# Two decode layers with cached attention: the fold's sums on GpSimd, a thinned chain, and unread products on TensorE behind its norms

## The chip, the cores and the metric

The kernel runs on one core of one Trainium2 chip. The metric is device time in microseconds (us) from launch to the end; lower is better. The core has TensorE (PE; its weight loads are listed apart as PEld), VectorE (DVE), ScalarE (ACT), GpSimd (POOL) and SyncE (SP), which here issues all the loads. Each engine takes its instructions in program order, and semaphores order them between engines. The stated time is the median of 3 runs.

## The reference

Eight sequences (B = 8) decode one token with D = 512. The same pair of blocks is applied twice, with the same weights and the same key and value caches. The caches are bf16 of 8 x 8 x 8192 x 128; a (sequence, head) pair holds 2 MB of keys and 2 MB of values.

```
def _A_ref(x, k_cache, v_cache, wq, wo):
    q = (lambda x, *d: x.transpose(*d))((x @ wq).reshape(B, Sq, Hq, Dh), 0, 2, 1, 3)   # 32 heads of 128
    k = jnp.repeat(k_cache, rep, axis=1)                                               # 8 cached heads, rep = 4
    v = jnp.repeat(v_cache, rep, axis=1)
    scores = jnp.einsum("bhqd,bhkd->bhqk", q, k) * (Dh ** -0.5)
    p = _softmax(scores, axis=-1)
    o = jnp.einsum("bhqk,bhkd->bhqd", p, v)
    return (lambda x, *d: x.transpose(*d))(o, 0, 2, 1, 3).reshape(B, Sq, Hq * Dh) @ wo

def _B_ref(x, w1, w2):                                                                 # 512 -> 1792 -> 512
    return jnp.einsum("bsf,fd->bsd", _silu(jnp.einsum("bsd,df->bsf", x, w1)), w2)

x = A_x
x = x + _A_ref(_layernorm(x, axis=-1), A_k_cache, A_v_cache, A_wq, A_wo)
x = x + _B_ref(_layernorm(x, axis=-1), B_w1, B_w2)
x = x + _A_ref(_layernorm(x, axis=-1), A_k_cache, A_v_cache, A_wq, A_wo)
x = x + _B_ref(_layernorm(x, axis=-1), B_w1, B_w2)
return x
```

## The kernel before

**Tasks.** One task is the attention of one sequence over one cached head in one layer: 128 tasks. `make_tasks` (L146) writes their order down. Of each sequence's eight heads, three (heads 0 to 2) have their keys loaded in both layers; five (heads 3 to 7, the 20 "kept" granules) keep their keys in SBUF from the first layer to the second. The order for a sequence b is: its five kept tasks of layer 0; then five or six other tasks, namely layer-1 tasks of heads 0 to 2 of the sequence before and layer-0 tasks of heads 0 to 2 of the sequences to come; then its five kept tasks of layer 1, which load values alone.

**Chain.** Between the kept tasks of layer 0 and those of layer 1 stands the *chain* of sequence b (`chain_of`, L808): the last wo heads, the residual, a layer norm, w1, silu, w2, the residual, the next layer norm and wq, for one sequence alone. It is a list of small stages.

**Positions.** A task is eight positions (p) of the loop at L857; two positions make a granule of 512 KB of keys or values. Each position emits, in this order: the queries of a task about to begin (`emit_q`), the transposes of key granules up to p + LT (`emit_t`, a VectorE transpose in place), at odd p the score products (`emit_s`, PE, L543), at odd p the products with the values of the granule LP = 14 positions back (`emit_pv`, PE, L608), the fold's steps, the softmax steps of the task before by phase p % 8 (`soft`, L843: maximum at 0, shift and exp at 2, sum at 4, transposes of P at 5, reciprocal at 7), then stages of the chain, or (outside the kept tasks of layer 1) one wo head, then `emit_norm`, and the loads whose slot the planner has free by then. The number of chain stages in a position is the number left over the number of positions left until EARLY = 4 before the first layer-1 kept task, rounded up (L881). Positions order the instructions on each engine; they set no time of their own.

**Loads.** The arena has 27 slots of 512 KB. `plan_loads` (L177) gives each granule a due position and a slot: keys are due LT positions before their first score products, values when `emit_pv` reads them. SP issues them in the order of their due positions and waits for the last reader of the slot. With 20 slots kept, seven circulate.

**Fold.** PV leaves in a PSUM bank (OTp) 128 x 512 partial results, of which each partition owns one of four blocks of 128 columns. `emit_own` (L621, at the position after the last PV, p - LP - 8) copies them to E: for 88 tasks by one ScalarE copy (L624), and for the 40 kept tasks of layer 1 (`eased`) by four VectorE instructions that multiply with the 0/1 column own_x and add (L629, L632). `emit_fold` (L636, two positions later) sums across partitions on PE in fp32: four products with `sel` for a ScalarE copy (eight PE instructions in the profile, L640), one with `hm` for an eased task (two PE instructions, L645). `emit_norm` (three positions after `emit_own`) scales on VectorE. E exists once; OTp, P^T (PT), scores (SCp) and the PSUM bank of the transposes (TPp, NTP = 2) twice. All eight PSUM banks are used.

**Layer norm.** `ln_stages` (L658) has three stages: the sum over the partition's elements on VectorE and the sum across partitions on GpSimd; centring, squares and sum on VectorE, then GpSimd again; variance, a bit-trick seed, three Newton steps and the scaling on VectorE (L685 to L699 for one sequence). In a chain two empty stages (`idle`, SETTLE = 2) follow each norm. `project` (L714) emits w1 and w2 in two pieces of 56 products and wq in four of 32.

Of the kernel before, what the change touches and what calls it, by code (L numbers as in the profile page):

```python
# [5 lines left out]
HQ = 32  # L6
DH = 128
SM_SCALE = DH ** -0.5
LN_EPS = 1e-5
RSQRT_SEED = float(0x5F3759DF)  # L10
# [6 lines left out]
KEEP = 20  # L17
LT = 2
PRE = 10
LP = 14  # L20
EARLY = 4
WO_FROM = 36
NTP = 2
NSCP = 2
# [8 lines left out]
PAIR_ALL = False  # L33
FOLD = 3
FOLD_AT = 2
ACT_FOLD = True
NQS = 4
CW = 32
SETTLE = 2

# [183 lines left out]
def _build(ctx, nc, A_x, A_k_cache, A_v_cache, A_wq, A_wo, B_w1, B_w2, out):  # L224
# [28 lines left out]
    def sb(shape, dt, name):  # L253
        _cnt[0] += 1
        return ctx.enter_context(nc.sbuf_tensor(f"{name}_{_cnt[0]}", shape, dt))
# [38 lines left out]
    s1 = sb([128, B], FP32, "s1")  # L294
    s1a = sb([128, B], FP32, "s1a")
    xc = sb([128, KT, B], FP32, "xc")
    sq = sb([128, KT, B], FP32, "sq")
# [25 lines left out]
    TPp = [ps_bank("TPp", BF16) for _ in range(NTP)]  # L323
    MISC = ps_bank("MISC")
    QSp = ps_bank("QSp")

# [60 lines left out]
    with nc.Block() as block:  # L387

        @block.sync
        def _(sync_eng):  # L390
# [184 lines left out]
            def softmax_sum(ti):  # L575
                st = ti % NST
                op(dve, lambda: dve.tensor_scalar(  # L577
                    ssm[st][:, :], hm[:, :], rs[st][:, 0:1], None, op0=ALU.mult),
                   reads=["hm", f"rs{st}"], writes=[f"ssm{st}"])
                op(pool, lambda: pool.partition_all_reduce(ssa[st][:, :], ssm[st][:, :], 128, bass.bass_isa.ReduceOp.add),  # L580
                   reads=[f"ssm{st}"], writes=[f"ssa{st}"])
# [34 lines left out]

            def eased(ti):
                layer, _b, g = tasks[ti]
                return layer == 1 and (g, 0) in kept

            def emit_own(ti):  # L621
                ob = ti % 2
                if not eased(ti) and ACT_FOLD:
                    op(act, lambda: act.copy(E[:, :], OTp[ob][:, :]), reads=[f"OT{ob}"], writes=["E"])  # L624
                    return
                for x in range(CPB):
                    ot = OTp[ob][:, x * DH:(x + 1) * DH]
                    if x == 0:
                        op(dve, lambda: dve.tensor_scalar(E[:, 0:DH], ot, own_x[:, 0:1], None, op0=ALU.mult),  # L629
                           reads=[f"OT{ob}", "own_x"], writes=["E"])  # L630
                    else:
                        op(dve, lambda x=x, ot=ot: dve.scalar_tensor_tensor(  # L632
                            E[:, 0:DH], ot, own_x[:, x:x + 1], E[:, 0:DH], op0=ALU.mult, op1=ALU.add),
                           reads=[f"OT{ob}", "own_x", "E"], writes=["E"])

            def emit_fold(ti):  # L636
                ob = ti % 2
                if not eased(ti) and ACT_FOLD:
                    steps = [
                        lambda x=x: pe.matmul(OTp[ob][:, 0:REP], E[:, x * DH:(x + 1) * DH], sel[:, x, :],  # L640
                                              start=(x == 0), stop=(x == CPB - 1))
                        for x in range(CPB)
                    ]
                else:
                    steps = [lambda: pe.matmul(OTp[ob][:, 0:REP], E[:, 0:DH], hm[:, :], start=True, stop=True)]  # L645
                mm_group(steps, reads=["E", "hm", "sel"], writes=[f"OT{ob}"])
# [11 lines left out]
            def ln_stages(xv, rx, n):  # L658

                xcv, sqv, xnv = xc[:, :, 0:n], sq[:, :, 0:n], xnT[:, :, 0:n]  # L660

                def first():
# [19 lines left out]
                def third():  # L682
# [7 lines left out]
                       reads=["yr"], writes=["yr"])  # L690
                    if n == 1:
                        scale = 1.0
                        for _n in range(NEWTON):
                            op(dve, lambda: dve.tensor_scalar(t, y, y, v, op0=ALU.mult, op1=ALU.mult),  # L694
                               reads=["yr", "vr"], writes=["tr"])
                            op(dve, lambda: dve.tensor_scalar(y, t, -3.0 * scale ** 2, y, op0=ALU.add, op1=ALU.mult),  # L696
                               reads=["tr", "yr"], writes=["yr"])
                            scale *= -2.0 * scale ** 2
                        op(dve, lambda: dve.tensor_scalar(xnv, xcv, y, 1.0 / scale, op0=ALU.mult, op1=ALU.mult),  # L699
                           reads=["xc", "yr"], writes=["xnT"])  # L700
                        return
                    for _n in range(NEWTON):
# [56 lines left out]

            settle = [idle] * SETTLE  # L760

            def block_stages(xs, rxs, n, fine=False):

                x0, x1, x2 = xs
                r0, r1, r2 = rxs
                parts = 2 if fine else 1

# [11 lines left out]
                def attended():  # L779
                    add_residual(x1, r1, x0, r0, n, CW if n == 1 else n)  # L780

                st = [attended] + ln_stages(x1, r1, n) + settle
                st += joined(project(w1_sb, "w1", FT, KT, lambda k: xnT[:, k, 0:n], "xnT", n, parts), expo)
                st += [silu, idle]
                st += joined(
                    project(w2_sb, "w2", KT, FT, lambda k: hsT[:, k * n:(k + 1) * n], "hsT", n, parts),
                    lambda: add_residual(x2, r2, x1, r1, n, n))
                return st

# [9 lines left out]
            def query(n, dst_of, rdst, parts=1):  # L799
                return joined(  # L800
                    project(wq_sb, "wq", HQ, KT, lambda k: xnT[:, k, 0:n], "xnT", n, parts),
                    lambda: op(
                        dve,
                        lambda: dve.tensor_copy(dst_of, MISC[:, 0:HQ * n].rearrange("p (h b) -> p h b", b=n)),
                        reads=["MISC"], writes=rdst,
                    ))

            def chain_of(b):  # L808
                xs = [XT[n][:, :, b:b + 1] for n in range(3)]
                st = block_stages(xs, ["XT0", "XT1", "XT2"], 1, True)  # L810
                st += ln_stages(xs[2], "XT2", 1) + settle
                return st + query(1, QT2[b % 2][:, 0:HQ].rearrange("p (h b) -> p h b", b=1), [f"QT2_{b % 2}"], 4)

# [41 lines left out]
            ntask = len(tasks)  # L855

            for p in range(NG + LP + GPT + FOLD + 1):  # L857
                tq = (p + LQ) // GPT
# [7 lines left out]
                if p % GPG == GPG - 1 and p < NG:  # L866
                    emit_s(p)
                if p % GPG == GPG - 1 and 0 <= p - LP < NG:
                    emit_pv(p - LP)
# [10 lines left out]
                if chain:  # L880
                    left = max(1, first1[chain_b[0]] - EARLY - p)  # L881
                    for _n in range(-(-len(chain) // left)):
                        chain.pop(0)()
                elif p >= WO_FROM and heads[turn[0]] and not (p < NG and tasks[p // GPT][0] and (tasks[p // GPT][2], 0) in kept
                                             and turn[0] < B):
                    add_heads(turn[0])
# [63 lines left out]
```

## Time and profile before

| What | Value |
|---|---|
| median of 3 runs (lowest to highest) | 1202.7 us (1202.06 to 1204.01) |
| the profiled execution's own time | 1203.2 us |
| its span, first to last instruction | 1201.2 us |
| mean granted TensorE clock | 0.600 |
| busy share PE, PEld, DVE, ACT, POOL | 68%, 42%, 61%, 23%, 10% |
| loaded by the program's queue | 465.12 MB, 99.2% of the span |
| L466 DVE key transposes | 352 of 1240 ns, 436.0 us |
| L608 PE products with the values | 2048 of 549 ns, 283.0 us |
| L543 PE score products | 7040 of 301 ns, 275.6 us |
| L640 PE fold after a ScalarE copy | 704 of 333 ns, 147.9 us |
| L624 ACT copy to E | 88 of 592 ns, 52.1 us |
| L629, L632 DVE to E, eased tasks | 40 of 323 ns, 120 of 351 ns, 55.0 us |
| L577 DVE ssm | 128 of 202 ns, 25.9 us |
| L721 PE w1, w2, wq (wq shown) | 1152 of 185 ns, 35.5 us |

The span is one execution under the hardware profiler; its own time lies 2.0 us over the span. A group's busy time is the union of its instructions; PE's overlap, so 549 ns a product is not what a row of them costs. The rate (GB/s) is what the 16 DMA engines moved in a slice or window, and the clock is TensorE's granted share of full speed.

### The profile page before, as it was taken

Reading aid. Unit: us, or ns where it says so; the run is one execution under the profiler, and the core shown is the slowest. Engines: PE = TensorE matmul, PEld = TensorE weight load, DVE = VectorE, ACT = ScalarE, POOL = GpSimd, SP = SyncE. Lnnn points to the kernel's source line nnn. Section 1 sums busy time; section 2 is a strip of 40 time slices with the busy share of each in tenths; the row PEclk is TensorE's granted clock in tenths of the full one; section 3 lists DMA queues with packets and bytes.
Section 4 is the critical chain, followed back from the end, with each engine's and each line's share of the span. In section 5 each row is a group of like instructions: output and inputs, shape, how many; then the busy total and the mean of one; then the engine's idle time right before and its main releaser. Section 6 shows DMA issues by size and latency. Waiting matters only on the chain.

```text
span 1201.2 us, 32533 instructions
## 1 busy us (share of the span) xinstructions
PE 811.5 (68%) x13960; PEld 505.4 (42%) x13960; DVE 735.7 (61%) x1858; ACT 274.0 (23%) x482; POOL 117.9 (10%) x300
## 2 busy tenths in 40 slices
PE   1537777576856686677757786667757676667865
PEld 1324444344524463345424454345434453345534
DVE  3736665767575655667476756657466756667472
ACT  0212123122312223221312132122312232121321
POOL 0000111001100111001100111001100111001100
PEclk9655576555855576555855566556755676555665
DMA  9999999999999999999999999999999999999993
GB/s 363 385 396 407 399 376 409 408 403 379 396 409 408 392 357 410 408 399 383 400 409 403 393 391 409 409 392 365 403 408 397 365 396 409 408 404 385 385 409 133
DMA packets 131568, 467.19 MB, mean 389 GB/s; under 512 B 13904, under 2 KB 19808, under 8 KB 130912
## 3 DMA queue, kind: packets, MB, share of 16 engines
q1 hardware_dynamic: 131424, 465.12, 99.2%
q8 instruction: 109, 1.79, 0.6%
q14 instruction: 35, 0.29, 0.1%
HBM read 465.05 MB, written 0.01 MB: 387 GB/s over the span
## 4 chain that ended last, share of the span: by engine, by line
DMA 59%; PE 15%; SPq 15%; DVE 7%; issue 3%; ACT 1%; POOL 1%; POOLq 0%; ACTq 0%; DVEq 0%
DMA arena<-in_A_v_cache_dram 48%; SPq L356 15%; DMA arena<-in_A_k_cache_dram 10%; PE OTp L608 5%; PE OTp L640 3%; PE MISC L721 3%; DVE arena L466 3%; PE SCp L543 3%; ACT P L570 1%; PE TPp L589 1%; DVE E L632 1%; DVE tr L694 1%; DVE yr L696 1%; DVE rowmax L554 0%; PE MISC L739 0%
## 5 line engine op out<-in xcount | busy, mean ns | idle before, releaser
L466 DVE STREAM_TRANSPOSE arena<-arena 128x1024 int32<-128x1024 int32 x352 | 436.0, 1240 | 239.1 <-DMA arena<-in_A_k_cache_dram 238.8
L608 PE MATMUL OTp<-arena,PT 128*16 128x512 bf16 x2048 | 283.0, 549 | 292.8 <-DMA arena<-in_A_v_cache_dram 289.9
L570 ACT ACTIVATE P<-SCp,shift 128x512 bf16<-128x512 f32 x128 | 180.4, 1409 | 646.2 <-PE SCp L543 234.1
L543 PE MATMUL SCp<-arena,QB 128*32 128x128 bf16 (+1 forms) x7040 | 275.6, 301 | 3.7 <-DVE mine L563 2.3
L608 PEld LDWEIGHTS OTp<-arena,PT 128*16 128x16 bf16 x2048 | 54.9, 97 | 383.6 <-DMA arena<-in_A_v_cache_dram 375.6
L543 PEld LDWEIGHTS SCp<-arena,QB 128*32 128x32 bf16 x7040 | 167.6, 122 | 63.8 <-issue 41.3
L640 PEld LDWEIGHTS OTp<-sel,E 128*128 128x128 f32 x704 | 140.3, 296 | 37.8 <-issue 25.6
L640 PE MATMUL OTp<-sel,E 128*128 128x4 f32 x704 | 147.9, 333 | 0.9 <-ACT E L624 0.7
L559 POOL PARTITION_ALL_REDUCE tops<-top x128 | 47.5, 371 | 563.1 <-DVE QT L655 241.6
L580 POOL PARTITION_ALL_REDUCE ssa<-ssm x128 | 55.2, 432 | 444.9 <-DVE ssm L577 423.4
L554 DVE TENSOR_REDUCE rowmax<-SCp 128x1 f32<-128x512 f32 x128 | 84.6, 661 | 21.4 <-PE SCp L543 20.9
L593 ACT COPY PT<-TPp 128x256 bf16<-128x256 bf16 x128 | 47.6, 372 | 211.7 <-PE TPp L589 211.7
L589 PE MATMUL TPp<-ident,P 128*128 128x128 bf16 x512 | 70.2, 283 | 12.4 <-ACT P L570 11.8
L589 PEld LDWEIGHTS TPp<-ident,P 128*128 128x128 bf16 x512 | 39.7, 121 | 66.2 <-issue 38.4
L577 DVE TENSOR_SCALAR ssm<-hm,rs 128x4 f32<-128x4 f32 x128 | 25.9, 202 | 66.5 <-ACT P L570 66.5
L624 ACT COPY E<-OTp 128x512 f32<-128x512 f32 x88 | 52.1, 592 | 4.1 <-PE OTp L608 4.1
L739 PEld LDWEIGHTS MISC<-at,wo 128*128 128x128 bf16 x1024 | 33.0, 105 | 34.2 <-DVE at L655 28.8
L721 PE MATMUL MISC<-xnT,wq 128*128 128x32 bf16 (+1 forms) x1152 | 35.5, 185 | 16.9 <-DVE xnT L708 15.7
L632 DVE SCALAR_TENSOR_TENSOR E<-OTp,own_x,E 128x128 f32<-128x128 f32 x120 | 42.1, 351 | 4.3
L721 PEld LDWEIGHTS MISC<-xnT,wq 128*128 128x128 bf16 x1152 | 34.4, 105 | 24.4 <-issue 22.1
L739 PE MATMUL MISC<-at,wo 128*128 128x32 bf16 x1024 | 38.2, 187 | 6.6 <-issue 1.3
L645 PE MATMUL OTp<-hm,E 128*128 128x4 f32 x80 | 20.5, 327 | 24.1 <-DVE E L632 24.1
(61 smaller groups left out, 359.3 us busy)
## 6 DMA issues: line engine op xcount, KB each, us to landing
arena<-in_A_v_cache_dram SPq DMA_DIRECT2D x512, 512.0 KB, 11.2
arena<-in_A_k_cache_dram SPq DMA_DIRECT2D x352, 512.0 KB, 14.9
wq<-in_A_wq_dram SPq DMA_DIRECT2D x1, 4096.0 KB, 16.4
wo<-in_A_wo_dram SPq DMA_DIRECT2D x1, 4096.0 KB, 26.0
w<-in_B_w_dram SPq DMA_DIRECT2D x2, 1792.0 KB, 22.6
P<-in_A_x_dram SPq DMA_DIRECT2D x1, 8.0 KB
out_dram<-P SPq DMA_DIRECT2D x1, 8.0 KB
```

The costliest lines, as they stand in the source:

```text
L356: eng.dma_start(out_ap, in_ap).then_inc(counter.sem, 16)
L466: op(dve, lambda: dve.transpose(words, words), reads=[r_half(slot, 0), r_half(slot, 1)], writes=[r_half(slot, 0), r_half(slot, 1)])
L543: lambda n=n, t=t, lo=lo, hi=hi, of=of: pe.matmul(SCp[bank][t * QUAD:(t + 1) * QUAD, lo * 128:hi * 128], QB[qn][:, n, :], of(t, n), start= ...
L554: op(dve, lambda: dve.tensor_reduce(rowmax[:, :], SCp[bank][:, :], AX.X, ALU.max), reads=[f"SC{bank}"], writes=["rowmax"])
L570: op(act, lambda: act.activation(P[:, :].rearrange("p (x j k) -> p k x j", x=CPB, k=NGRAN), SCp[bank][:, :].rearrange("p (k x j) -> p k x ...
L580: op(pool, lambda: pool.partition_all_reduce(ssa[st][:, :], ssm[st][:, :], 128, bass.bass_isa.ReduceOp.add), reads=[f"ssm{st}"], writes=[f ...
L589: lambda c=c: pe.transpose(tpv[:, c, :], P[:, c * 128:(c + 1) * 128], ident[:, :])
L608: lambda t=t: pe.matmul(OTp[ob][t * QUAD:t * QUAD + CPB * REP, :], PT[pb][:, k, t].rearrange("p x r -> p (x r)"), ARENA[:, slot * SLOT + t ...
L632: op(dve, lambda x=x, ot=ot: dve.scalar_tensor_tensor(E[:, 0:DH], ot, own_x[:, x:x + 1], E[:, 0:DH], op0=ALU.mult, op1=ALU.add), reads=[f" ...
L640: lambda x=x: pe.matmul(OTp[ob][:, 0:REP], E[:, x * DH:(x + 1) * DH], sel[:, x, :], start=(x == 0), stop=(x == CPB - 1))
L721: lambda o=o, k=k: pe.matmul(MISC[:, o * n:o * n + w], w_sb[:, k, o * 128:(o + 1) * 128], rhs_of(k).to_broadcast([128, w]) if n == 1 else ...
L739: lambda o=o, h=h: pe.matmul(MISC[:, o * w:(o + 1) * w], wo_sb[:, h, o * 128:(o + 1) * 128], rhs_of(h).to_broadcast([128, w]) if n == 1 el ...
```

## The change

The constants shift the pipeline: keys are transposed and due one position later (LT 2 to 1), PV comes one position earlier and so at even p (LP 14 to 13), the fold comes four instead of two positions after `emit_own`, the norm five instead of three. One TPp bank is given up for a bank VOID.

Every task's partial results but the last one's are now copied to E by ScalarE; GpSimd then multiplies E (128 x 512, fp32) by own_x and adds halves twice (256 and 128 columns), and PE sums across partitions with one product. The last task keeps the ScalarE copy and the four products.

The small product ssm moves from VectorE to ScalarE. In a chain's norms the sums go to ScalarE (with its accumulator), the centring, the Newton steps and the scaling to GpSimd; three VectorE instructions stay. A norm's first stage joins the residual's stage (`along`). wq's copy moves to ScalarE. Behind each of the two norms of a chain stand four stages instead of two, and each holds FILL = 2 products of 512 columns with resident operands into VOID, which nothing reads.

wo heads of sequence b are added only from the position of its first kept task of layer 0 on (`calm`), no longer in the tasks before. The final norm and block, for all eight sequences together, keep their VectorE form.

```diff
--- before.py
+++ after.py
...
 KEEP = 20
-LT = 2
+LT = 1
 PRE = 10
-LP = 14
+LP = 13
 EARLY = 4
 WO_FROM = 36
-NTP = 2
+NTP = 1
+FILL = 2
 NSCP = 2
...
 PAIR_ALL = False
-FOLD = 3
-FOLD_AT = 2
-ACT_FOLD = True
+FOLD = 5
+FOLD_AT = 4
+PIECES = (2, 2, 4)
 NQS = 4
 CW = 32
-SETTLE = 2
+SETTLE = 4
 
...
     s1a = sb([128, B], FP32, "s1a")
+    s2 = sb([128, 1], FP32, "s2")
+    s2a = sb([128, 1], FP32, "s2a")
     xc = sb([128, KT, B], FP32, "xc")
...
     MISC = ps_bank("MISC")
+    VOID = ps_bank("VOID")
     QSp = ps_bank("QSp")
...
                 st = ti % NST
-                op(dve, lambda: dve.tensor_scalar(
-                    ssm[st][:, :], hm[:, :], rs[st][:, 0:1], None, op0=ALU.mult),
+                op(act, lambda: act.activation(ssm[st][:, :], hm[:, :], ACT.Copy, scale=rs[st][:, 0:1]),
                    reads=["hm", f"rs{st}"], writes=[f"ssm{st}"])
...
 
-            def eased(ti):
-                layer, _b, g = tasks[ti]
-                return layer == 1 and (g, 0) in kept
+            def straight(ti):
+                return ti == len(tasks) - 1
 
...
                 ob = ti % 2
-                if not eased(ti) and ACT_FOLD:
-                    op(act, lambda: act.copy(E[:, :], OTp[ob][:, :]), reads=[f"OT{ob}"], writes=["E"])
+                op(act, lambda: act.copy(E[:, :], OTp[ob][:, :]), reads=[f"OT{ob}"], writes=["E"])
+                if straight(ti):
                     return
-                for x in range(CPB):
-                    ot = OTp[ob][:, x * DH:(x + 1) * DH]
-                    if x == 0:
-                        op(dve, lambda: dve.tensor_scalar(E[:, 0:DH], ot, own_x[:, 0:1], None, op0=ALU.mult),
-                           reads=[f"OT{ob}", "own_x"], writes=["E"])
-                    else:
-                        op(dve, lambda x=x, ot=ot: dve.scalar_tensor_tensor(
-                            E[:, 0:DH], ot, own_x[:, x:x + 1], E[:, 0:DH], op0=ALU.mult, op1=ALU.add),
-                           reads=[f"OT{ob}", "own_x", "E"], writes=["E"])
+                ev = E[:, :].rearrange("p (x d) -> p x d", d=DH)
+                op(pool, lambda: pool.tensor_tensor(
+                    ev, ev, own_x[:, :].unsqueeze(2).to_broadcast([128, CPB, DH]), ALU.mult),
+                   reads=["E", "own_x"], writes=["E"])
+                n = CPB * DH // 2
+                while n >= DH:
+                    op(pool, lambda n=n: pool.tensor_tensor(E[:, 0:n], E[:, 0:n], E[:, n:2 * n], ALU.add),
+                       reads=["E"], writes=["E"])
+                    n //= 2
 
...
                 ob = ti % 2
-                if not eased(ti) and ACT_FOLD:
+                if straight(ti):
                     steps = [
...
                 xcv, sqv, xnv = xc[:, :, 0:n], sq[:, :, 0:n], xnT[:, :, 0:n]
+
+                def one_first():
+                    op(act, lambda: act.activation(sqv, xv, ACT.Copy, scale=-1.0 / D, accum_out=s1[:, 0:1]),
+                       reads=[rx], writes=["sq", "s1"])
+                    op(pool, lambda: pool.partition_all_reduce(s1a[:, 0:1], s1[:, 0:1], 128, bass.bass_isa.ReduceOp.add),
+                       reads=["s1"], writes=["s1a"])
+
+                def one_second():
+                    op(act, lambda: act.activation(sqv, xv, ACT.Square, bias=s1a[:, 0:1], accum_out=s2[:, 0:1]),
+                       reads=[rx, "s1a"], writes=["sq", "s2"])
+                    op(pool, lambda: pool.tensor_scalar(
+                        xcv, xv, s1a[:, 0:1], -2.0 ** -13, op0=ALU.add, op1=ALU.mult),
+                       reads=[rx, "s1a"], writes=["xc"])
+                    op(pool, lambda: pool.partition_all_reduce(s2a[:, 0:1], s2[:, 0:1], 128, bass.bass_isa.ReduceOp.add),
+                       reads=["s2"], writes=["s2a"])
+
+                def one_third():
+                    v, y, t = vr[:, 0:1], yr[:, 0:1], tr[:, 0:1]
+                    vi, yi = v.bitcast(INT32), y.bitcast(INT32)
+                    op(dve, lambda: dve.tensor_scalar(v, s2a[:, 0:1], 1.0 / D, LN_EPS, op0=ALU.mult, op1=ALU.add),
+                       reads=["s2a"], writes=["vr"])
+                    op(dve, lambda: dve.tensor_scalar(yi, vi, 1, None, op0=ALU.logical_shift_right),
+                       reads=["vr"], writes=["yr"])
+                    op(dve, lambda: dve.tensor_scalar(yi, yi, -1.0, RSQRT_SEED, op0=ALU.mult, op1=ALU.add),
+                       reads=["yr"], writes=["yr"])
+                    scale = 1.0
+                    for _n in range(NEWTON):
+                        op(pool, lambda: pool.tensor_scalar(t, y, y, v, op0=ALU.mult, op1=ALU.mult),
+                           reads=["yr", "vr"], writes=["tr"])
+                        op(pool, lambda scale=scale: pool.tensor_scalar(
+                            y, t, -3.0 * scale ** 2, y, op0=ALU.add, op1=ALU.mult),
+                           reads=["tr", "yr"], writes=["yr"])
+                        scale *= -2.0 * scale ** 2
+                    assert scale == -2.0 ** 13
+                    op(pool, lambda: pool.tensor_scalar(xnv, xcv, y, None, op0=ALU.mult),
+                       reads=["xc", "yr"], writes=["xnT"])
+
+                if n == 1:
+                    return [one_first, one_second, one_third]
 
...
                        reads=["yr"], writes=["yr"])
-                    if n == 1:
-                        scale = 1.0
-                        for _n in range(NEWTON):
-                            op(dve, lambda: dve.tensor_scalar(t, y, y, v, op0=ALU.mult, op1=ALU.mult),
-                               reads=["yr", "vr"], writes=["tr"])
-                            op(dve, lambda: dve.tensor_scalar(y, t, -3.0 * scale ** 2, y, op0=ALU.add, op1=ALU.mult),
-                               reads=["tr", "yr"], writes=["yr"])
-                            scale *= -2.0 * scale ** 2
-                        op(dve, lambda: dve.tensor_scalar(xnv, xcv, y, 1.0 / scale, op0=ALU.mult, op1=ALU.mult),
-                           reads=["xc", "yr"], writes=["xnT"])
-                        return
                     for _n in range(NEWTON):
...
 
-            settle = [idle] * SETTLE
+            def spin():
+                mm_group([lambda: pe.matmul(VOID[:, :], ident[:, :], w1_sb[:, 0, 0:512], start=True, stop=True)] * FILL,
+                         reads=["ident", "w1"], writes=["VOID"])
+
+            settle = [spin] * SETTLE
 
...
                 r0, r1, r2 = rxs
-                parts = 2 if fine else 1
+                p1, p2 = PIECES[:2] if fine else (1, 1)
 
...
 
-                st = [attended] + ln_stages(x1, r1, n) + settle
-                st += joined(project(w1_sb, "w1", FT, KT, lambda k: xnT[:, k, 0:n], "xnT", n, parts), expo)
+                st = along([attended], ln_stages(x1, r1, n)) + (settle if fine else [])
+                st += joined(project(w1_sb, "w1", FT, KT, lambda k: xnT[:, k, 0:n], "xnT", n, p1), expo)
                 st += [silu, idle]
-                st += joined(
-                    project(w2_sb, "w2", KT, FT, lambda k: hsT[:, k * n:(k + 1) * n], "hsT", n, parts),
+                return st + joined(
+                    project(w2_sb, "w2", KT, FT, lambda k: hsT[:, k * n:(k + 1) * n], "hsT", n, p2),
                     lambda: add_residual(x2, r2, x1, r1, n, n))
-                return st
+
+            def along(stages, more):
+                return stages[:-1] + joined(stages[-1:], more[0]) + more[1:]
 
...
                     lambda: op(
-                        dve,
-                        lambda: dve.tensor_copy(dst_of, MISC[:, 0:HQ * n].rearrange("p (h b) -> p h b", b=n)),
+                        *((act, lambda: act.copy(dst_of, MISC[:, 0:HQ * n].rearrange("p (h b) -> p h b", b=n)))
+                          if n == 1 else
+                          (dve, lambda: dve.tensor_copy(dst_of, MISC[:, 0:HQ * n].rearrange("p (h b) -> p h b", b=n)))),
                         reads=["MISC"], writes=rdst,
...
                 st = block_stages(xs, ["XT0", "XT1", "XT2"], 1, True)
-                st += ln_stages(xs[2], "XT2", 1) + settle
-                return st + query(1, QT2[b % 2][:, 0:HQ].rearrange("p (h b) -> p h b", b=1), [f"QT2_{b % 2}"], 4)
+                st = along(st, ln_stages(xs[2], "XT2", 1)) + settle
+                return st + query(1, QT2[b % 2][:, 0:HQ].rearrange("p (h b) -> p h b", b=1), [f"QT2_{b % 2}"], PIECES[2])
 
...
 
+            kept_from = min(g for g, _k in kept)
+
+            def calm(p):
+                if p >= NG:
+                    return False
+                return p >= task_at[(0, turn[0], kept_from)] * GPT
+
             for p in range(NG + LP + GPT + FOLD + 1):
...
                     emit_s(p)
-                if p % GPG == GPG - 1 and 0 <= p - LP < NG:
+                if (p - LP) % GPG == GPG - 1 and 0 <= p - LP < NG:
                     emit_pv(p - LP)
...
                         chain.pop(0)()
-                elif p >= WO_FROM and heads[turn[0]] and not (p < NG and tasks[p // GPT][0] and (tasks[p // GPT][2], 0) in kept
-                                             and turn[0] < B):
+                elif p >= WO_FROM and heads[turn[0]] and (turn[0] == B or calm(p)):
                     add_heads(turn[0])
...
```

## The prediction, made before the result was known

> **What bounds the kernel now.** I read the page's slices first, then the busy windows of one batch, then the chain of waits, then the timeline of a layer norm.
>
> The slices: the profiled execution is cut into 40 slices of 30 us.
>
> ```profile
> PE   1537777576856686677757786667757676667865
> PEclk9655576555855576555855566556755676555665
> GB/s 363 385 396 407 399 376 409 408 403 379 396 409 408 392 357 410 408 399 383 400 409 403 393 391 409 409 392 365 403 408 397 365 396 409 408 404 385 385 409 133
> ```
>
> The transfer rate sits at 408 to 410 GB/s and never above, and dips once per batch element. 465.12 MB at 409 GB/s are 1137 us; the span is 1201.2. Summing (1 - rate/409) x 30.03 over the slices gives 59 us: 5 in the first two, 20 in the last (the end, when nothing is left to load), 33 in the dips. Only the dips and the end can be won. A window for each of the eight dips (127:182, 260:316, 393:450, 527:581, 659:716, 791:847, 925:981, 1068:1119) shows 388, 383, 375, 385, 389, 376, 374 and 380 GB/s; the same sum over them is 30 us, 2.8 to 4.8 each, 3.75 on average.
>
> One dip in pieces (batch element 3; columns: length, busy us of PE, PEld, DVE, ACT, POOL, clock, DMA share, GB/s):
>
> ```profile
> 485.80:516.50 30.70, 20.01 (x306) 11.70 (x302) 20.23 (x40) 6.31 (x12) 2.40 (x6) 0.50 1.03 408
> 516.50:536.90 20.40, 14.54 (x220) 8.94 (x216) 12.69 (x24) 4.55 (x9) 1.60 (x4) 0.50 1.02 398
> 536.90:558.70 21.80, 15.38 (x270) 10.39 (x262) 15.70 (x42) 4.70 (x9) 2.42 (x6) 0.50 1.01 387
> 558.70:570.30 11.60, 9.56 (x233) 7.51 (x233) 9.07 (x27) 2.31 (x5) 1.59 (x4) 0.65 1.00 379
> 570.30:581.40 11.10, 9.27 (x204) 5.93 (x196) 4.89 (x18) 4.53 (x8) 1.61 (x4) 0.96 0.99 381
> 581.40:598.10 16.70, 13.58 (x204) 6.95 (x200) 8.01 (x32) 5.85 (x10) 2.40 (x6) 0.71 1.03 410
> ```
>
> Full rate at first; 398 in the last two kept tasks; 387 and 379 where the chain (residual, norm, w1, w2, norm, wq) runs between the attention tasks, PE at 70 to 82%; 381 in the two fast tasks after; full rate again once tasks need V alone. A load is 512 KB, 1.28 us at 409. The chain of waits tells how many are under way:
>
> ```profile
> 506.72 14.59 DMA arena<-in_A_v_cache_dram
> ...
> 522.05 6.86 DMA arena<-in_A_v_cache_dram
> ```
>
> 14.59 us from issue to landing is 11 loads in flight, 6.86 is 5. In the tight stretch only seven slots circulate, so any engine that frees a slot late takes a load out of flight. That is the bound: slots coming free late while the chain runs. The timeline of the first norm:
>
> ```profile
> 549.80 0.60 PE L608 MATMUL OTp<-arena,PT 128*16 128x512 bf16 x4 [1.52 <-DMA arena<-in_A_v_cache_dram]
> ...
> 552.18 0.24 DVE L699 TENSOR_SCALAR xnT<-xc,yr 128x4 bf16<-128x4 f32 x1
> ...
> 552.46 1.23 DVE L466 STREAM_TRANSPOSE arena<-arena 128x1024 int32<-128x1024 int32 x1
> ...
> 552.48 1.72 PE L721 MATMUL MISC<-xnT,w 128*128 128x32 bf16 x56 [1.54 <-DVE xnT L699]
> ...
> 555.11 1.87 PE L640 MATMUL OTp<-sel,E 128*128 128x4 f32 x8
> ```
>
> PE idles 1.54 us for xnT, a key transpose stands behind the Newton steps, and the fold takes PE for 1.87 us.
>
> **The change, part by part**, per dip, in us of engine time:
>
> (a) Fold. Eight fp32 products become two, the form that L645 has now for 40 tasks:
>
> ```profile
> L640 PE MATMUL OTp<-sel,E 128*128 128x4 f32 x704 | 147.9, 333 | 0.9 <-ACT E L624 0.7
> ...
> L645 PE MATMUL OTp<-hm,E 128*128 128x4 f32 x80 | 20.5, 327 | 24.1 <-DVE E L632 24.1
> ```
>
> 8 took 1.80 to 1.87, so 0.23 each; six fewer save 1.35 a task. Some 3.5 tasks of the slow pieces had the eight: -4.7.
>
> (b) Norm. Ten VectorE instructions from vr to xnT ran 549.95 to 552.43, 2.5 us; three stay, seven go to GpSimd, where the trace shows no such operation: from 0.1 each (its 128x1 memset) to 0.43 (its all-reduce) gives 0.7 to 3.0; I take 2.0. Two or four settle positions of 1.28 us lie over it, so it reaches PE no more. The table of waits has 9.3 us of PEld L721 behind xnT L699 in 16 norms: -1.2 a dip. Transposes no longer queue behind Newton: -0.5 (0 to -2).
>
> (c) Unread products: eight positions a chain, two each, 16. One alone is not in the trace. Below: 0, where PE waits for V anyway (1.52 above). Above: 0.55, L608's mean for 128x512, so 8.8. L589 puts four 128-column products in 0.61, 0.15 per 128, at the 0.50 clock; the issue rate inside is nearer 0.10, so 0.4 for 512 and 6.4 for 16. PE is idle some 20% of the stretch; half hides: +3.
>
> (d) Clock. Four PV products take 0.60 at clock 0.50 (549.80) and 0.39 at 1.00 (561.00); four PT products 0.61 and 0.40; sixteen score products 0.62 and 0.42. That is 4 x 0.2 + 4 x 0.21 + 0.21 = 1.9 a task. The rows show 0.50 at two thirds busy and 0.96 at 84%, so filled positions should hold it up for most of one more task: -1.5 (0 to -3.8). The Trainium skill, "TensorE: Matmul & The Clock Gate", Part 1, has the array at full clock after one busy window of some 3.4 us and at half after an idle one; the rows agree. By that rule alone the four products of the first two settle positions would lift the clock for two tasks, -3.8, and the sum below would be about 1185.
>
> (e) GpSimd sums, 127 tasks: 512, 256 and 128 elements, 7 x 128. Below 1.0 (ScalarE's 0.592 copy of 512, scaled); above 3.2 (the 0.282 affine select x7, and 0.4 overhead on each of three); I take 2.0, the select x7. E copy 0.59, sums 2.0, handovers 0.1 make 2.7. Four positions lie between own and fold: 5.1 at 10.24 a task, hidden; 2.2 to 2.6 in the two fast tasks, so up to 0.5 of PE waiting. There, too, the E copy now stands ahead of the PT copy that PV needs one position later: 0.59. Twice 1.1: +2.2. If GpSimd were held up, its all-reduces queue behind the sums, then exp, then PT.
>
> (f) At nothing: one TPp bank (its last reader ran a task earlier); LT and LP, which shift K, PV and the loads' order on SP together (K and V still alternate, a slot is held from landing to the same reader; PV swaps places with one score group; without that cover at most one load, 1.28 a dip); ssm on ScalarE (0.2, 23% busy); the 55 us that E took on VectorE in kept layer-1 tasks (there the rate is full); heads held back to calm positions (0.6 each, moved to where 11 loads fly). Chain positions: 24 stages in 17 positions against 22 in 18, so w1 and w2 often come two pieces at once, a burst of 3.44; that is within (c)'s range.
>
> Sum: -4.7 -1.7 +3 -1.5 +2.2 = -2.7 a dip. But without the chain the stretch would still run at the kept tasks' 398: 2.7% of 55 us, 1.5, is a floor, so of 3.75 at most 2.25 is to be had, less in shallow dips: I take 1.6, x8 = 13. At the end, the last fold but one (1.87 at 1180.5) stands ahead of the last PV: -1. So -14 from the profiled 1203.2 (span 1201.2 and 2.0 around it): 1189.2, and as that execution lay 0.5 over the median 1202.7, **1189**.
>
> **Rivals.**
> - Wider gain: floor halves too, 25 won: 1178. For it: 32 us lie open. Chance 0.14.
> - Nothing gained: products at 0.55 each on PE and the clock down: +8.8 for +3, 0 for -1.5, the dip grows back: 1202 (1199 to 1206). For it: PE is 82% busy there. Against it: idle behind V. Chance 0.12.
> - Slower: GpSimd's sums too long. PE is in order, so a late fold holds scores and PV and thereby slots. Each us over 2.0 costs 2 us a dip in the fast tasks; from 3.4 nothing is gained; at 4.4 it is (4.8 - 2.7) x 8 = +17: 1220. Against it: the select's 0.282. Chance 0.13.
> - Slower: Square needs another function table than Exp. Now one load of 1.28 us stands ahead of all (L570 ACT_TABLE_LOAD x1); two loads at each of 16 norms, 2.6 ahead of exp, 5.1 a dip, half hidden: -14 + 20 = +6: 1209. Chance 0.04.
> - Shared port: a VectorE op with two SBUF operands (top 0.22, mine 0.13) held by one sum (4 x 0.282 = 1.1) in each fast task: 16 x 1.1, half of it kept: 1198. That is the rule of the Trainium skill, "SBUF — State Buffer", "Who interferes with whom"; no run here shows it, as GpSimd now has no such sums. Chance 0.07.
>
> Forecast 0.50, own range 1183 to 1197. Faster by over 0.2% (below 1200.3; 0.2% is about what a measurement tells from no change): 0.50 + 0.14 + 0.07 + 0.02 = 0.73. Within: 0.08. Slower: 0.17 + 0.02 = 0.19. Range 1177 to 1207, which leaves out the long sums and the table.
>
> **What would show it.** Right: the dips at 395 or more; fold at two products, under 0.5; no PE wait behind xnT; the clock at 1.00 over w1 and w2; POOL's three sums at 2 us together. Wrong: PE L645's successor waiting on POOL by several us a task; ACT_TABLE_LOAD beside the norms; the dips as deep as now with PE over 90% busy; or new dips in the kept layer-1 tasks.

## The result and the profile after

The changed kernel takes 2855.4 us (median of 4 runs, 2839.6 to 2858.1) against 1202.4 before: 2.372 times as long, with a 95% interval of 2.363 to 2.381. The profiled execution's span is 2853.4 us, its mean clock 0.544.

The page's slices of the kernel after (each is now 71 us):

```profile
PE   2322223232232223222232322322232223223223
POOL 1111111111111111111111111111111111111111
PEclk9855555555555555555555555555555555555555
GB/s 375 253 197 111 185 206 116 165 114 226 162 140 146 138 225 120 169 115 173 207 114 167 111 228 163 140 148 140 218 123 182 105 185 193 124 170 126 192 177 1
```

From the third slice to the last but one the rate is 105 to 228 GB/s, and every task is hit, not only those beside a chain. No engine is busy for more than 28% of the span, GpSimd for 15%. The chain of work that ended last, as shares of the span, says the same, here before and after:

```profile
DMA 59%; PE 15%; SPq 15%; DVE 7%; issue 3%; ACT 1%; POOL 1%; POOLq 0%; ACTq 0%; DVEq 0%
```

```profile
issue 69%; POOL 13%; PE 6%; DVE 6%; ACT 5%; DMA 1%; POOLq 0%; ACTq 0%; DVEq 0%
```

The transfers have left the chain: the kernel is no longer bound by them.

The page's costliest groups (busy us, mean ns, then the idle time in front of them and what ended it):

```profile
L567 DVE SCALAR_TENSOR_TENSOR mine<-tops,hm 128x4 f32<-128x4 f32 x128 | 20.8, 162 | 1579.1 <-POOL tops L563 1579.1
L647 PE MATMUL OTp<-hm,E 128*128 128x4 f32 x254 | 74.8, 365 | 953.1 <-POOL E L634 953.1
...
L629 POOL TENSOR_TENSOR E<-E,own_x 128x512 f32<-128x512 f32 x127 | 130.8, 1030 | 925.7 <-issue 925.7
...
L563 POOL PARTITION_ALL_REDUCE tops<-top x128 | 49.4, 386 | 772.7 <-issue 758.2
```

VectorE and PE wait for GpSimd, and GpSimd waits for "issue": nothing that the profile shows as work. This is one of the signs of being wrong that the prediction named: the fold's product waits for GpSimd by 8 us a task (953.1 us in 119 waits). One task of the timeline tells where (the copy to E, an all-reduce, the elementwise sums, the next all-reduce):

```profile
511.76 0.57 ACT L625 COPY E<-OTp 128x512 f32<-128x512 f32 x1
...
511.96 0.44 POOL L583 PARTITION_ALL_REDUCE ssa<-ssm  x1 [2.35 <-ACT ssm L581]
...
521.46 1.03 POOL L629 TENSOR_TENSOR E<-E,own_x 128x512 f32<-128x512 f32 x1 [9.06 <-issue]
522.56 1.26 POOL L634 TENSOR_TENSOR E<-E 128x256 f32<-128x256 f32 x2
523.87 0.59 PE L647 MATMUL OTp<-hm,E 128*128 128x4 f32 x2 [9.01 <-POOL E L634]
...
529.67 0.39 POOL L563 PARTITION_ALL_REDUCE tops<-top  x1 [5.86 <-issue]
530.09 0.16 DVE L567 SCALAR_TENSOR_TENSOR mine<-tops,hm 128x4 f32<-128x4 f32 x1 [13.94 <-POOL tops L563]
```

The three sums take 2.3 us together. In front of them stand 9.06 us, though their operand E was ready 0.07 us before the gap began (511.76 + 0.57 against 511.96 + 0.44); behind them stand 5.86. The view of line L563 names what stands in the gap, an instruction of GpSimd's sequencer that counts as no work:

```profile
L563 POOLq MODIFY_POOL_CONFIG  x252: 11/11/11, 54.4 to 2816.2; - x126
```

These come in pairs: one pair in front of the setup's first select, and one wherever GpSimd passes from an all-reduce to an elementwise operation or back. Over all lines there are 608 of them after (304 pairs) and 4 before (2 pairs). The idle time ended by "issue" on GpSimd's lines L629, L563, L583, L690, L673, L676 and L706 is 2061 us in 302 gaps, 6.8 us each. They are not all alike: in front of elementwise work after an all-reduce they are 6.6 to 11.9 us (median 7.2), in front of an all-reduce after elementwise work 5.7 to 8.5 (median 5.9).

**Theory (reload):** the two kinds of GpSimd work do not stand ready together; each change from one to the other costs 6 to 12 us, 6.8 on average, whatever the size of the operation. **Rivals:** the sums themselves are too long for an engine whose results PE and VectorE wait for in order; or the shared port of the prediction's last rival.

### The profile page after: what moved, and what is told of

Read it like the earlier page. It is cut to its first block, busy times and chain, and to the rows that moved or that the text cites. A ratio compares the mean times of both kernels' runs of the same rounds, so it can differ in the third digit from the quotient of the medians.

```text
span 2853.4 us, 33330 instructions
## 1 busy us (share of the span) xinstructions
PE 810.7 (28%) x13838; PEld 465.5 (16%) x13838; DVE 625.0 (22%) x1386; ACT 333.0 (12%) x722; POOL 439.2 (15%) x809
## 4 chain that ended last, share of the span: by engine, by line
issue 69%; POOL 13%; PE 6%; DVE 6%; ACT 5%; DMA 1%; POOLq 0%; ACTq 0%; DVEq 0%
POOL E L634 5%; POOL E L629 4%; ACT P L574 3%; DVE arena L470 3%; POOL tops L563 2%; PE SCp L547 2%; PE TPp L592 1%; ACT PT L596 1%; PE MISC L751 1%; PE OTp L611 1%; ACT E L625 1%; PE MISC L769 1%; DVE mine L567 1%; DVE shift L570 1%; POOL tr L690 1%
## 5 line engine op out<-in xcount | busy, mean ns | idle before, releaser
L547 PE MATMUL SCp<-arena,QB 128*32 128x128 bf16 (+1 forms) x7312 | 307.6, 320 | 397.4 <-DVE arena L470 359.5
L567 DVE SCALAR_TENSOR_TENSOR mine<-tops,hm 128x4 f32<-128x4 f32 x128 | 20.8, 162 | 1579.1 <-POOL tops L563 1579.1
L647 PE MATMUL OTp<-hm,E 128*128 128x4 f32 x254 | 74.8, 365 | 953.1 <-POOL E L634 953.1
L611 PE MATMUL OTp<-arena,PT 128*16 128x512 bf16 x2048 | 313.8, 601 | 63.5 <-ACT PT L596 41.5
L547 PEld LDWEIGHTS SCp<-arena,QB 128*32 128x32 bf16 x7312 | 210.9, 134 | 532.6 <-DVE arena L470 403.6
L629 POOL TENSOR_TENSOR E<-E,own_x 128x512 f32<-128x512 f32 x127 | 130.8, 1030 | 925.7 <-issue 925.7
L647 PEld LDWEIGHTS OTp<-hm,E 128*128 128x128 f32 x254 | 63.7, 312 | 1002.7 <-POOL E L634 1001.1
L563 POOL PARTITION_ALL_REDUCE tops<-top x128 | 49.4, 386 | 772.7 <-issue 758.2
L634 POOL TENSOR_TENSOR E<-E 128x256 f32<-128x256 f32 x254 | 149.6, 589 | 19.9
L583 POOL PARTITION_ALL_REDUCE ssa<-ssm x128 | 56.5, 442 | 315.6 <-ACT ssm L581 264.1
L625 ACT COPY E<-OTp 128x512 f32<-128x512 f32 x128 | 72.4, 566 | 11.4 <-PE OTp L611 11.3
L791 PE MATMUL VOID<-w,ident 128*128 128x512 bf16 x128 | 58.5, 575 | 0.0
```

The source lines that it names most:

```text
L547: lambda n=n, t=t, lo=lo, hi=hi, of=of: pe.matmul(SCp[bank][t * QUAD:(t + 1) * QUAD, lo * 128:hi * 128], QB[qn][:, n, :], of(t, n), start= ...
L563: op(pool, lambda: pool.partition_all_reduce(tops[:, :], top[:, :], 128, bass.bass_isa.ReduceOp.max), reads=["top"], writes=["tops"])
L611: lambda t=t: pe.matmul(OTp[ob][t * QUAD:t * QUAD + CPB * REP, :], PT[pb][:, k, t].rearrange("p x r -> p (x r)"), ARENA[:, slot * SLOT + t ...
L629: op(pool, lambda: pool.tensor_tensor(ev, ev, own_x[:, :].unsqueeze(2).to_broadcast([128, CPB, DH]), ALU.mult), reads=["E", "own_x"], writ ...
L634: op(pool, lambda n=n: pool.tensor_tensor(E[:, 0:n], E[:, 0:n], E[:, n:2 * n], ALU.add), reads=["E"], writes=["E"])
```

## Experiments: is it the change of kind?

**One operation of one element.** The kernel before, with this in `emit_own`:

```diff
+ op(pool, lambda: pool.tensor_scalar(junk[:, 0:1], hm[:, 0:1], 2.0, None, op0=ALU.mult), ...)
```

> The kernel before, with one unread GpSimd elementwise operation of 128x1 added to each task where the fold's copy is emitted. Theory (reload): GpSimd runs the all-reduces and the elementwise operations from two sets of code, and each change from one to the other costs what the profile after shows in front of them, 7.2 us from an all-reduce to an elementwise operation and 5.9 us back, whatever the size. Then a task's GpSimd loop is 0.4 + 0.4 + 7.2 + 0.3 + 5.9 = 14.2 us, and the exp that the next all-reduce waits for adds some 2.5: about 16.5 us a task, 2100 us in all (1850 to 2300). Rival (long sums: the three sums themselves, 2.3 us a task, and the port that they share with VectorE hold PE and VectorE up): an operation of one element costs nothing, 1203 us.

Measured: 2457 us (one run), above the stated 2300. Rows from the views of its line and of the next all-reduce, then that all-reduce's idle time (us, times):

```profile
L624 POOLq MODIFY_POOL_CONFIG  x254: 82/85/85, 43.6 to 2428.7; - x127
L624 POOL TENSOR_SCALAR junk<-hm x128: 209/261/262, 50.9 to 2436.2; 128x1 f32<-128x1 f32 x128
```

```profile
L560 POOLq MODIFY_POOL_CONFIG  x248: 5/7/7, 51.4 to 2420.0; - x124
...
  issue: 965.5, 124
```

An unread operation of 0.26 us in each task, whose result nothing waits for, costs 1255 us. In front of it stand 968.6 us of "issue" in 127 gaps (7.6 each), in front of the next all-reduce 965.5 in 124 (7.8): more than the 7.2 and 5.9 assumed. Over 127 tasks that is some 290 of the 360 us by which the time lies over 2100; the rest was not traced. "Long sums" is refuted as the main cause.

**Another all-reduce, and a memset, in the same place.**

```diff
+ op(pool, lambda: pool.partition_all_reduce(junk[:, :], hm[:, :], 128, bass.bass_isa.ReduceOp.add), ...)
```

> The kernel before, with one unread GpSimd all-reduce of 128x4 added to each task at the same place. Theory (reload): no change of code set, 0.43 us more on an engine that is 10% busy, so 1203 us (1199 to 1207). Rival (any further instruction between the two all-reduces of a task delays the softmax): about 128 x 0.4 = 50 us more, 1250 us.

```diff
+ op(pool, lambda: pool.memset(junk[:, 0:1], 2.0), writes=["junk"])
```

> The kernel before, with one unread GpSimd memset of 128x1 added to each task at the same place. At the start of the kernel before, two memsets follow an elementwise select without a gap, and one precedes it. If a memset needs the elementwise code set, the reload theory gives about 2100 us as for the elementwise operation; if a memset belongs to neither, 1203 us. The rival (long sums) gives 1203 us in any case.

Measured: 1200.6 us and 1203.0 us (one run each), beside 1202.1 for the kernel before. Neither shows a further configuration instruction. So it is not the number of instructions on GpSimd, and a memset costs no change.

**All the elementwise work, no all-reduce.** The kernel after, with one replacement in six places:

```diff
- pool.partition_all_reduce(OUT, IN, 128, bass.bass_isa.ReduceOp.add)
+ pool.tensor_scalar(OUT, IN, 1.0, None, op0=ALU.add)
```

> The kernel after, with each of its all-reduces replaced by a GpSimd elementwise addition of 1.0 of the same shape: the sums and maxima across partitions are left out, and GpSimd has one kind of work only. Theory (reload): no reload is left after the start, and the time is what the rest of the change makes: the blind forecast's 1189 us (1177 to 1207). Rival (long sums, or the port shared with VectorE): the sums of 512, 256 and 128 columns are all still there, and the time stays above 2000 us.

Measured: 1183.4 us, 0.985 times the kernel before (0.982 to 0.987). It leaves out the sums and maxima across partitions, so its output is not the reference's; it shows a time alone. In its timeline the three sums and what stands for the next all-reduce follow each other with no gap over 0.1 us:

```profile
544.56 1.04 POOL L629 TENSOR_TENSOR E<-E,own_x 128x512 f32<-128x512 f32 x1
...
545.67 1.29 POOL L634 TENSOR_TENSOR E<-E 128x256 f32<-128x256 f32 x2
...
546.95 0.22 POOL L563 TENSOR_SCALAR tops<-top 128x4 f32<-128x4 f32 x1
```

The sums of 512, 256 and 128 columns are all there (GpSimd 33% busy), and the time is below that of the kernel before: as causes of the slowdown both rivals fall. This kernel has a pair of configuration instructions too, at its start, and its first select follows less than 0.1 us behind a memset, where the kernel before waits 8.2: the instruction alone is not the price. The elementwise work alone gives 1183, the all-reduces alone 1199 (below), both together 2855: the alternation is what costs the 1653 us, to within those 15. The 1183 lies at the low end of the range of the forecast's own case (1183 to 1197), but for a kernel that it was not made for, and its parts came out otherwise (see "The other terms" below).

**The two halves of GpSimd's work.** The norms' part alone (fold as before) and the fold's part alone (norms on VectorE):

```diff
- emit_own, emit_fold of the kernel after
+ emit_own, emit_fold of the kernel before, FOLD_AT = 4
```

> The kernel after, with the fold of the kernel before (ScalarE copy and eight products on PE, or VectorE): of GpSimd's elementwise work only that of the sixteen norms is left. Theory (reload): four changes a norm (into the centring, out of it, into Newton, out of it), 7.2 + 6.0 + 7.1 + 5.8 = 26 us a norm, 64 changes and 416 us over the 1200 us that the same kernel takes with the norms on VectorE; what the other tasks' slack hides is taken off: 1450 to 1620 us. Rival (the reload is paid only in the loop of every task): below 1300 us.

```diff
- op(pool, lambda: pool.tensor_scalar(...))    # in one_second and one_third
+ op(dve, lambda: dve.tensor_scalar(...))
```

> The kernel after, with the norms' elementwise work on VectorE: of GpSimd's elementwise work only the fold's sums are left, 127 x 2 changes. Theory (reload): as with one operation of one element a task (2457 us) plus the sums' own 2.3 us where the next all-reduce waits behind them: 2500 to 2750 us, and with the norms' kernel the two add up to the 1652 us of the change. Rival (sums and norms disturb each other): the two parts add to less than half of it.

Measured: 1555.9 and 2533.7 us (one run each), both in their ranges. Against the same kernels without that GpSimd work (1200.1 and 1198.7, below), the 64 changes of the norms cost 356 us, 5.6 each, and the 254 of the fold 1335, 5.3 each. Together 1691, against 1657 for both at once (2855.4 against 1198.7): they add. Against the 6.8 of a gap in the kernel after, some 1.2 to 1.5 us of each change is hidden.

## Experiments: what the rest of the change is worth

**Without elementwise work on GpSimd, given to VectorE.** E as the kernel before makes it for its kept layer-1 tasks, norms as in the last diff; then the same with `settle = [idle] * SETTLE`.

> The kernel after, with all of GpSimd's elementwise work given to VectorE: E as the kernel before makes it for its kept layer-1 tasks (four instructions from PSUM, 1.38 us a task), and the norms' centring, Newton steps and scaling. GpSimd has all-reduces alone. Theory (reload): as without the all-reduces (1183 us), a little longer for VectorE's 1.38 us in each task of the dips: 1184 to 1194 us. A theory by which the later fold, the earlier PV or the chain's order cost time of their own gives more than 1202 us.

> The same with the unread products taken out (their positions stay, empty). By the blind prediction's terms the products cost 3 us a dip and bring back 1.5 by the clock, so that without them the time is shorter by some 4 us (0 to 12): 1180 to 1190 us. Rival: the clock is worth more than the products take; then it is longer by 2 us or more than with them.

Measured: 1198.7 us, 0.998 of before (0.996 to 0.999), and 1199.6, the same ratio. Both lie above their ranges, the gain is gone, and of the products neither the gain of 4 us nor the loss of 2 is seen. VectorE is busy for 68% of the span and for 43.1 of the 60 us from 520 to 580, against 61% and 40.1 before. That this is the reason is argued; the bf16 fold below, which takes E off VectorE (35.6 of the same 60 us) and changes the fold on PE with it, is 8 us faster.

**Fold as in the kernel before, on PE, norms on VectorE**, with and without the unread products:

> The kernel after, with the fold as the kernel before has it (ScalarE copy and eight fp32 products on PE, or VectorE for the kept layer-1 tasks) and the norms' elementwise work on VectorE: thinned chain, later positions and unread products remain. GpSimd has all-reduces alone. By the prediction's terms it lacks the 4.7 us a dip of the shorter fold, which is most of the gain: 1194 to 1203 us. If the fold's PE time is not what the dips come from, about 1185 us as with the sums on VectorE.

> The same without the unread products. By the prediction's terms 0 to 8 us shorter than with them: 1190 to 1200 us. Rival (the clock is worth more than the products take): 2 us or more longer than with them.

Measured: 1200.1 us (0.999 of before, 0.997 to 1.001), in its range, and 1211.4 (1.008, 1.006 to 1.010): here the expectation missed and its rival came true. The products are worth 11 us. The page's clock and rate, with them and without:

```profile
PEclk9999986656665588557665587558665677557665
GB/s 361 386 396 409 402 362 409 409 409 393 369 408 409 406 378 408 409 409 386 400 408 407 402 376 408 409 406 386 403 408 403 390 392 409 409 407 370 395 409 116
```

```profile
PEclk9995577555665567556665566555765577556655
GB/s 358 386 397 409 397 380 411 408 409 365 376 409 409 407 331 409 409 408 380 383 409 408 388 350 408 409 408 348 389 408 406 377 347 409 409 408 398 385 408 133
```

By the prediction's sum over the slices the dips are 26.7 us with the products and 41.7 without. The mean clock is 0.690 against 0.616, and in the 30 us from each chain's first norm on, averaged over the eight chains, 0.87 against 0.61. The products are the only difference between the two, so they are the cause; that they work through the clock, and that this pays here because the long fold keeps PE late, fits these numbers but was not separated from what their mere place in PE's order does.

The second of the two shows something else. It has the long fold and no products, and takes 10 us more than the kernel before (1201.4 beside it). So the rest of the change (later positions, one TPp bank, four empty settle positions, sums and ssm on ScalarE, heads held back), which the prediction put mostly at nothing, costs time with this fold, and the products only win it back. Which part of it costs was not tried.

**A bf16 fold.** ScalarE writes E in bf16 for every task, PE sums it with four products:

```diff
- E = sb([128, CPB * DH], FP32, "E")
+ E = sb([128, CPB * DH], BF16, "E")
- sel = sb([128, CPB, REP], FP32, "sel")
+ sel = sb([128, CPB, REP], BF16, "sel")
- ev = E[:, :]...                                # the three GpSimd sums and the single product
```

> The kernel after without any elementwise work on GpSimd: E is written by ScalarE in bf16 for every task, the four products of the fold run on bf16, and the norms' elementwise work is on VectorE. The partial sums are rounded to bf16 before they are added. Theory (the dips come from the engine time of the fold on PE and of E on VectorE): both are gone, four products of 128 columns of weights take some 0.4 us (a wo head's 16 take 0.6) and VectorE is freed of 55 us, so the time is that of the kernel without all-reduces or less: 1178 to 1190 us. Rival (only VectorE's norms matter): 1195 to 1203 us, as with the sums on VectorE.

> The same without the unread products. Without the long fold PE is less busy and the clock lower, as with the sums on VectorE, where the products made no difference that could be told (1198.7 with, 1199.6 without): the same time within 3 us, 1178 to 1193 us. Rival (the products are worth 11 us, as they were with the long fold): 1188 to 1204 us.

Measured: 1190.6 us (0.991 of before, 0.989 to 0.993) and 1188.9 (0.990, 0.988 to 0.992). The fold of the first, by shape:

```profile
L631 PE MATMUL OTp<-sel,E 128*128 128x4 bf16 x512 | 33.8, 170 | 1.2 <-ACT E L625 0.7 <-issue 0.5
```

33.8 us for 128 tasks are 0.26 a task, where the eight fp32 instructions took 1.7 by the same measure (147.9 for 88 tasks). The first lies a little over its range, the second in it, with the products making no difference outside the runs' spread. This version, with or without them, is some 1% faster than the kernel before. It rounds partial sums to bf16, which neither of the two does.

## Why the prediction was wrong, point by point

**The step that failed** is (e), and with it (b): both bounded an operation that the trace lacked by the *durations* of the nearest GpSimd rows ("below 1.0, above 3.2") and put the passage between kinds at nothing. The durations were nearly right: 2.3 us for the sums against 2.0 taken; 2.7 for the Newton steps and the scaling (in the kernel without all-reduces) against 2.0. What was missing is the gap on either side, 9.06 and 5.86 us in the task shown. So the overlap failed too: (e) hid 2.7 us from the copy to the end of the sums in 5.1 of slack, and they take 12.1 (511.76 to 523.82). The trace of before shows it, twice, in two rows of the table of waits that the working did not use:

```profile
POOL s1a L665 <- issue: 11.3, 1, 11.3
...
POOL ident L396 <- issue: 8.2, 1, 8.2
```

The second row stands in front of the setup's elementwise select, the first in front of the first all-reduce, the kernel's one change of kind; that all-reduce starts at 21.10, while its operand was ready at 11.73. The rows used for the price, the 0.282 of the select and the 0.43 of the all-reduce, are those instructions' own: their durations begin after the gap. At two changes a task, 7.2 and 5.9 by the gaps of the profile after, 127 tasks give 1660 us and the sixteen norms, at 26, another 416; of these 2080 us 1653 show in the time.

The Trainium skill states a price of this kind: "GPSIMD Engine Reference", section 2.1, says that GpSimd's code is loadable and that the first call to freshly loaded code pays some 6 us. The runs agree in size (5.7 to 11.9 us, median 6.8) and go further: it comes back at each change between all-reduce and elementwise work, as if each displaced the other's code, so that "first" comes twice a task. That the gaps are such loads is the reading that fits; the traces show the configuration instructions and the gaps, not what is loaded.

**The slower rival** had the right chain of effects (a late fold holds PE) and the wrong cause and size: it took sums of 4.4 us and 1220 us, and let them hurt the sixteen fast tasks alone. With the gap the sums take 11.4 us, the next all-reduce comes 5.9 after them, and every task is late.

**Square and its table**: the kernel after has one table load, at 34 us, and none beside the norms; that rival falls. **The shared port**: in the kernel without all-reduces the sums run in every task, and the time is 1183; a term of 9 us is not seen in that time, though it was not measured by itself.

**The other terms** can be read in that kernel, where reload is absent, with the reserve that it lacks the all-reduces too. Its dips, by the sum over the slices used in the prediction, are 12.9 us against 33.3 before: 20 won, where 13 was forecast and 18 (2.25 in each of eight dips) was the most it allowed. One of its dips:

```profile
537.40:549.30 11.90, 10.67 (x242) 6.71 (x234) 7.29 (x20) 3.54 (x12) 5.43 (x15) 0.76 1.03 406
549.30:558.00 8.70, 6.41 (x136) 3.32 (x129) 6.57 (x15) 2.64 (x8) 5.45 (x15) 1.00 1.01 397
558.00:566.50 8.50, 6.28 (x187) 4.31 (x183) 4.12 (x11) 2.72 (x6) 2.66 (x5) 1.00 1.02 409
```

The rate is 397 to 409 with the chain running, and the clock 1.00 where it was 0.65. In the 30 us from each chain's first norm on, averaged over the eight chains, the clock is 0.84 against 0.65; as it is only ever 0.50 or 1.00 in these traces, that is 11 us more at the full clock in each dip. So (d), which took most of one more task, was near, a little low: a task lasts about 10 us. The two tasks which the rule of the Trainium skill cited there would have given are not reached; and the rows of the prediction agree with that rule only in part, as the clock was at half with PE two thirds busy, not idle. The products of (c), four and then two:

```profile
541.06 1.91 PE L791 MATMUL VOID<-w,ident 128*128 128x512 bf16 x4
...
550.41 0.60 PE L791 MATMUL VOID<-w,ident 128*128 128x512 bf16 x2
```

Apart by some 0.43 us at the low clock and 0.21 at the full one: 0.4 was taken. (a) The two fp32 instructions took 0.59 at the low clock (in the kernel after) and 0.39 at the full one, where (a) took twice 0.23; it thus overstated the saving at the low clock a little, 1.28 a task and not 1.35. The floor of 1.5 us a dip was set about right: 12.9 over eight dips is 1.6. That the norms' chain reaches PE no more is seen there too: from 541.87 to 544.61 GpSimd's Newton steps run under the products, and over all sixteen norms PE's weight loads wait 0.3 us behind xnT. With the shorter folds, taking the products out changed nothing that could be measured, so neither the +3 of (c) nor the -1.5 of (d) shows in a time. Against (f), which put most of the rest of the change at nothing, stands the kernel with the long fold and no products: 10 us slower than before.

But (a) and (b) need not be had on GpSimd, and the last group of experiments shows that the place matters: with the fold's sums on VectorE most of what the shorter fold on PE wins is lost again (1198.7), and ScalarE plus a bf16 fold keep most of it (1188.9). The 7 us left between the bf16 fold with the products (1190.6) and 1183.4 lie in the norms on VectorE, in the all-reduces or in the two forms of the fold; which of them was not tried.

## What to carry to other kernels

Before an engine gets a new kind of operation, look in the trace not for how long such an operation lasts but for what stands in front of its first instance: an idle gap ended by "issue" can be a price that comes back at each change of kind, as it does here. On GpSimd, keep all-reduces and elementwise work out of the same loop; one 128x1 operation a task, added there, cost 1255 us. An engine that is 10% busy is not free if what it does next has to be loaded first.

## What the runs showed of the hardware

- A change between all-reduce and elementwise work on GpSimd leaves a gap of 5.7 to 11.9 us, mean 6.8 over 302 gaps, in the kernel after; with operands of 128x1 the means are 7.6 and 7.8, so the size of the operand does not matter. A memset needs none (1203.0 us). The configuration instructions themselves take at most 0.09 us, count as no busy time, and leave GpSimd at 15%.
- Unread products brought 11 us with the long fp32 fold on PE (1200.1 against 1211.4) and nothing measurable with shorter folds there (1198.7 and 1199.6; 1190.6 and 1188.9).
- Four bf16 products with 128 weight columns and 4 moving columns took 0.26 us a task, the fp32 form of the same fold 1.7.
